# Moving the attention of two token chunks later, and the gate's quadratic into its accumulator banks, in a fused attention and two-layer FFN kernel

## The chip, the core and the metric

The kernel runs on one core of a Trainium2 chip. The metric is the device time of one execution in microseconds (us), the median of several runs. TensorE (PE) multiplies matrices and writes PSUM, which has eight banks of 128x512 f32; VectorE (DVE), ScalarE (ACT) and GpSimd (POOL) do the rest; SyncE (SP) issues the DMAs.

## The reference, cut to what matters

```python
def _attn_ref(q, k, v, f_logit):              # 4 x 8 x 768 x 48
    f = 1.0 / (1.0 + np.exp(-f_logit))
    for t in range(S):
        state = f[:, :, t, :, None] * state + np.einsum('bhd,bhe->bhde', k[:, :, t], v[:, :, t])
        y[:, :, t] = np.einsum('bhd,bhde->bhe', q[:, :, t], state)

def _moe_ref(x, w_in, w_out, a, b):           # 3072 x 384 -> 2048 -> 384
    h = x @ w_in
    P = a[0] + a[1] * h + a[2] * h2 + a[3] * h3       # h2 = h*h, h3 = h2*h
    Q = 1.0 + np.abs(b[0]) * np.abs(h) + np.abs(b[1]) * h2
    return (P / (Q + 1e-06)) @ w_out

def _moe2_ref(x, domain_probs, w1, w2):       # 4 experts, 384 -> 1024 -> 384
    p = domain_probs / (domain_probs.sum(-1, keepdims=True) + 1e-09)
    for e in range(E):
        h = np.maximum(x @ w1[e], 0.0)
        out += p[:, e:e + 1] * (h @ w2[e])
```

A linear attention with a decaying state feeds a first FFN, whose activation is the quotient P/Q (the "gate"). Its result feeds a second FFN with four experts.

## The kernel before, in words

The 3072 tokens are cut into six chunks of 512 (c = 0 to 5), each of four blocks of 128 tokens (b = 0 to 3, one per batch row). The program is one loop over steps v (from -25 to 192). Chunk c's second FFN fills the 32 steps 32c to 32c+31 (four experts of eight tiles). A step holds, in this order on PE: "in2" of tile v+1 (9 matmuls, line L863, into one of two banks hb), "out2" of tile v-1 (9 matmuls, L873, summed in three banks acc), and, where the tables say so, a tile of the next chunk's first FFN: "in1" (9 matmuls into bank 5, called h1) and, four times a chunk, "out1" (36 matmuls, L873, into the same banks acc). All matrices are split into a high and a low part, hence three products for each.

Around them: relu(v) makes the high part of a tile on ACT (L983) and the low part on DVE (L984). With two hb banks, in2(v+2) at the start of step v+1 has to wait for L984 of tile v. gate_in is on ACT: a copy of the bank (L929), its square q (L933), r (L934) and y (L935). gate_step is on DVE, for the tile before (L944, L946 or L953, L958, L975) and for the new one (L949, L968, L970), with a Ln and an Exp on ACT (L950, L951) and a cast on ACT (L960). At the end of an expert evac2 takes the three acc banks (L1018 on DVE, L1019 on POOL); out1 follows it in the same banks, and evac1 adds its result (L1036). In the first steps, until about step 33, ACT and POOL also split weights into high and low parts (L819, L820).

The attention of chunk c, block b runs in six stages, in the steps t0(c, b)+1 to t0(c, b)+6. First stage: a decay on DVE (w, L431, and four scans, L438). Second: its inverse on ACT (L446, L447), the scaled key on POOL (L452), and a Newton correction on DVE (L457, L458, L462). Third: the scaled query on POOL (L467). Fourth: the scores on PE (L471) and their mask on DVE (L482). Fifth: L487 and L495 on PE. Sixth: the state's update on PE (L538), and L552 and L564 on DVE. From chunk 1's tiles on, the attention uses banks 6 and 7. When a chunk is finished, write_out transposes four blocks on PE (L1043), copies each on ACT (L1050) into one of two buffers (os), and sends it out by a DMA (L1052).

Nothing is reordered by a scheduler: each engine executes its instructions in the order in which this loop writes them. What sets that order are the numbers in first_mix_steps and t0.

Of the kernel before, what the change touches and what calls it, by code (L numbers as in the profile page):

```python
# [8 lines left out]
F32 = mybir.dt.float32  # L9
# [8 lines left out]
NB, NH, S, D = 4, 8, 768, 48  # L18
DM = NH * D
C = 128  # L20
NCH = S // C
# [324 lines left out]
def first_mix_steps():  # L346


    when, groups = {}, {}
    for c in range(1, NCH):  # L350
        p = NE * NJ2 * (c - 1)
        if c == 1:
            at = [10, 11, 12, 13, 14, 15, 16, 17, 18, 19, 20, 21, 23, 24, 25, 26]
            ends = (16, 20, 24, 29)
        else:
            at = [2, 3, 4, 5] if c == 2 else [-1, 1, 3, 5]
            at += [7, 9, 11, 13, 15, 17, 19, 21, 23, 24, 25, 26]
            ends = (8, 16, 24, 29)
        for j, s in enumerate(at):
            when[p + s] = (c, j)  # L360
        for n, s in enumerate(ends):
            groups[p + s] = (c, n)
    return when, groups
# [204 lines left out]
class Att:  # L568
# [16 lines left out]
    @staticmethod  # L585
    def t0(c, b):
        if c == 1:
            return -6 + 3 * b
        if c == 2:
            return (8, 14, 20, 26)[b]  # L590
        return NE * NJ2 * (c - 1) - (30, 24, 17, 9)[b]

    def start(self, fetch):
# [103 lines left out]
    def begin(self, v):  # L697
        ops = tuple([] for _ in range(7))
        for c in range(1, NCH):
            for b in reversed(range(NB)):  # L700
                k = v - self.t0(c, b)
                if 1 <= k <= 6:
                    for at, fs in self.stage(self.blocks[c, b], k).items():
                        ops[at].extend(fs)
        return ops
# [3 lines left out]
def fused(ctx, tc, aps, consts, gm, big, dp, prep, flag_op):  # L709
# [8 lines left out]
    acc, hb, h1 = banks[0:3], banks[3:5], banks[5]  # L718
# [206 lines left out]
    def gate_in(u):  # L925
        h = u[2]
        if u[0]:
            h = gp.tile([128, 512], F32, tag="h", name="h")
            nc.scalar.copy(out=h, in_=u[2])  # L929
        q = gp.tile([128, 512], F32, tag="q", name="q", bufs=3) if u[0] else banks[5 + u[1] % 2]  # L930
        r = gp.tile([128, 512], F32, tag="r", name="r")
        y = gp.tile([128, 512], F32, tag="y", name="y")
        nc.scalar.activation(out=q, in_=h, func=AF.Square)  # L933
        nc.scalar.activation(out=r, in_=h, func=AF.Abs, scale=sc[:, 4:5])  # L934
        nc.scalar.activation(out=y, in_=h, func=AF.Identity, scale=sc[:, 0:1], bias=sc[:, 1:2])  # L935
        return q, r, y, h
# [104 lines left out]
    def write_out(c, b, bank):  # L1041
        for m in range(3):
            nc.tensor.transpose(bank[:, m * C:(m + 1) * C], o[c][:, m, b * C:(b + 1) * C], ident)  # L1043
        if c == NCH - 1:
            if not last:
                last.append(sp.tile([128, NB, DM], F32, tag="s1", name="os"))
            nc.scalar.copy(out=last[0][:, b], in_=bank[:, 0:DM])
            return
        t = osp.tile([128, DM], F32, tag="os", name="os")
        nc.scalar.copy(out=t, in_=bank[:, 0:DM])  # L1050
        r0 = b * S + c * C
        nc.sync.dma_start(out=out[r0:r0 + C, :], in_=t)  # L1052
# [12 lines left out]
    for v in range(-FILL - 6, LAST + 1):  # L1065
        tau = v + FILL
        ops = att.begin(v)
        if tau == -4:
            prep()
        if tau + 6 <= NB:  # L1070
            att.first(tau + 6, conv_ops(tau), fetch, partial(fill_in, 0, 0, NB - 1))
        run_late()
        store_all()
        items = steps.get(v, [])
        lead = 1 if items and items[0][0] == "in2" and items[0][1] == v + 1 else 0
        fill_run(ops[PA], 9 * lead)
        for item in items[:lead]:
            emit(item)
        if 0 <= v < LAST and v not in act2:
            relu(v)  # L1080
        for f in ops[ACT0]:
            f()
        for u in gate_queue:
            if u[0] and u[:2] not in gate:
                gate[u[:2]] = gate_in(u)
        if 0 <= tau + 1 < NJ1:
            fill_in(tau + 1, (NB - 1) * (tau < 0))
        ready = [u for u in gate_queue if u[:2] in gate]
        new = ready[0] if ready else None
        if new:  # L1090
            gate_queue.remove(new)
        old, pend_old = pend_old, new
        if new or old:
            gate_step(new, old, ops)
        else:
            for f in ops[DVE1] + ops[ACT1] + ops[POOL1]:
                f()
        c, k = v // (NE * NJ2) - 1, v % (NE * NJ2)
        if v in (LAST - 4, LAST - 3):
            for b in range(2):  # L1100
                write_out(NCH - 1, b + 2 * (v - LAST + 4), banks[6 + b])
        if 0 <= c < NCH - 1 and k == 2:
            for b in range(2):
                write_out(c, b + (2 if c else 0), banks[6 + b])
        fill_run(ops[PB], 9 * any(item[0] == "out2" for item in items), True)
        for item in items[lead:]:
            if item[0] == "out2":
                emit(item)
                if run_bounds(v - 1)[1]:
                    evac2(v - 1)  # L1110
        for item in items[lead:]:
            if item[0] == "in2":
                emit(item)
                if v + 1 < LAST:
                    relu(v + 1)
        if 0 <= c < NCH - 1 and k == (1 if c else 2):
            for b in range(2):
                write_out(c, b + (0 if c else 2), banks[6 + b])
        for item in items[lead:]:
            if item[0] == "out1":  # L1120
                emit(item)
        for item in items[lead:]:
            if item[0] == "in1":
                emit(item)
        for u in gate_queue:
            if not u[0] and u[:2] not in gate:
                gate[u[:2]] = gate_in(u)
        if tau == -1:
            spread_probs()
        if 0 <= tau - 2 < NJ1:  # L1130
            fill_out(tau - 2)
        for f in ops[REST]:
            f()
        if v in groups:
            evac1(*groups[v])
        if tau + 6 > NB:
            for f in sum(conv_ops(tau), []):
                f()
            run_late()
        if 10 <= tau and v < -1:  # L1140
            make_ready(min(R - 6, 2 * (tau - 9)))
            split_to(min(AHEAD, state["ready"] - 2))
        if tau == NJ1 + 1:
            for m in range(3):
                split_x2(0, m, acc[m], nc.vector)
            load_pb(0)
        if v >= -1:
            split_to(state["used"] + AHEAD)
        att.loads(v)
        if v == 170:  # L1150
            flag_op(banks[6], banks[7])
# [178 lines left out]
```

## Time and profile before

| | us |
|---|---|
| median of 3 runs | 1368.79 (1368.64 to 1369.47) |
| the profiled execution | 1367.35 |
| its span in the trace | 1365.5 |
| PE busy in the span | 1325.7 (97%) |
| DVE busy | 870.5 (64%) |
| ACT busy | 663.1 (49%) |
| POOL busy | 287.6 (21%) |

The profiled execution took 1.85 us around its span, and was 1.44 us under the median. A row of the trace's timeline gives the start, the duration, the engine, the line, what is written from what, the count, and in brackets how long the engine had been idle and what it waited for. Line numbers are those of the kernel before.

### The profile page before, as it was taken

The numbers are of one execution on the slowest core, as the hardware profiler recorded it, in microseconds if no ns is written. First come the engines' busy times: TensorE is split into PE (matmuls) and PEld (weight loads), VectorE is DVE, ScalarE is ACT, GpSimd is POOL, SyncE is SP. The second block draws the span as 40 slices with busy tenths as digits, with TensorE's granted clock in tenths as the row PEclk, the third lists the DMA queues.
The fourth block names the chain that finished last, engine by engine and source line by source line (L and its number), as shares of the span: only waits on it lengthen the run. The fifth ranks groups of instructions, "written<-read, shape, count | busy, mean of one in ns | idle before, by whom it ended". The sixth has DMA issues, their size and how long they took to land.

```text
span 1365.5 us, 19581 instructions
## 1 busy us (share of the span) xinstructions
PE 1325.7 (97%) x7152; PEld 1060.7 (78%) x7152; DVE 870.5 (64%) x1367; ACT 663.1 (49%) x1152; POOL 287.6 (21%) x257
## 2 busy tenths in 40 slices
PE   7899999898899999999999999999999999999998
PEld 6444788777788888888888888888888888888887
DVE  7999659677748576757666757576575465552221
ACT  3897448666536545525545535553445453431111
POOL 0133555566420020120110111001111000111010
PEclk9999999999999999999999999999999999999999
DMA  8547877667875666667656758665657676667660
GB/s 298 199 174 260 284 259 263 223 242 254 301 255 176 207 219 189 188 207 228 221 166 204 227 166 267 198 208 186 216 176 243 191 196 195 192 192 239 195 195 28
DMA packets 115706, 291.03 MB, mean 213 GB/s; under 512 B 13105, under 2 KB 28817, under 8 KB 114833
## 3 DMA queue, kind: packets, MB, share of 16 engines
q1 hardware_dynamic: 115024, 289.51, 65.9%
q8 instruction: 59, 0.97, 0.3%
q14 instruction: 47, 0.38, 0.1%
q10 hardware_dynamic: 576, 0.18, 0.1%
HBM read 240.83 MB, written 48.81 MB: 212 GB/s over the span
## 4 chain that ended last, share of the span: by engine, by line


## 5 line engine op out<-in xcount | busy, mean ns | idle before, releaser
L863 PE MATMUL bank<-x,w 128*128 128x512 f32 x2448 | 595.1, 391 | 6.7 <-DVE gl L984 6.7
L863 PEld LDWEIGHTS bank<-x,w 128*128 128x128 f32 x2448 | 457.2, 188 | 103.9 <-DVE gl L984 8.8
L873 PE MATMUL bank<-gh,w 128*128 128x512 f32 x1584 | 495.0, 394 | 6.6 <-DVE t L1018 6.6
L873 PEld LDWEIGHTS bank<-gh,w 128*128 128x128 f32 x1584 | 295.5, 189 | 73.2 <-DVE t L1018 7.9
L873 PE MATMUL bank<-gl,w 128*128 128x512 f32 x792 | 309.8, 391 | 0.0
L984 DVE SCALAR_TENSOR_TENSOR gl<-bank,gh 128x512 fp32r<-128x512 f32 x192 | 131.4, 685 | 154.5 <-ACT gh L983 154.2
L1019 POOL TENSOR_TENSOR o<-o,t 128x512 f32<-128x512 f32 x69 | 88.9, 1317 | 529.1 <-DVE t L1018 529.1
L873 PEld LDWEIGHTS bank<-gl,w 128*128 128x128 f32 x792 | 149.3, 189 | 31.3
L983 ACT ACTIVATE gh<-bank 128x512 fp32r<-128x512 f32 x192 | 113.7, 593 | 122.6 <-PE bank L863 122.6
L949 DVE SCALAR_TENSOR_TENSOR q<-q,sc,r 128x512 f32<-128x512 f32 x80 | 61.6, 770 | 141.8 <-ACT r L934 141.8
L960 ACT CAST gh<-q 128x512 fp32r<-128x512 f32 x80 | 49.2, 615 | 186.7 <-DVE q L958 186.6
L820 POOL TENSOR_TENSOR w<-rawbuf,w 128x384 fp32r<-128x384 f32 x96 | 104.5, 1113 | 88.6 <-ACT w L819 74.2
L929 ACT COPY h<-bank 128x512 f32<-128x512 f32 x80 | 46.8, 585 | 114.6 <-PE bank L863 113.9
L1036 DVE TENSOR_TENSOR s<-s,bank 128x512 f32<-128x512 f32 x45 | 31.0, 688 | 84.5 <-PE bank L873 84.4
L975 DVE TENSOR_TENSOR gl<-q,gh 128x512 fp32r<-128x512 f32 x80 | 55.9, 699 | 33.8 <-ACT gh L960 33.6
L950 ACT ACTIVATE r<-q,sc 128x512 f32<-128x512 f32 x80 | 58.0, 725 | 25.1 <-DVE q L949 18.4
L944 DVE SCALAR_TENSOR_TENSOR q<-q,r 128x512 f32<-128x512 f32 x80 | 69.5, 868 | 0.1
L935 ACT ACTIVATE y<-h,sc 128x512 f32<-128x512 f32 x80 | 64.2, 803 | 0.0
L958 DVE SCALAR_TENSOR_TENSOR q<-y,sc,q 128x512 f32<-128x512 f32 x80 | 62.2, 778 | 1.8
L970 DVE SCALAR_TENSOR_TENSOR y<-y,sc,h 128x512 f32<-128x512 f32 x80 | 61.1, 764 | 2.8
L951 ACT ACTIVATE r<-r 128x512 f32<-128x512 f32 x96 | 60.7, 633 | 3.0
L968 DVE TENSOR_TENSOR y<-y,h 128x512 f32<-128x512 f32 x80 | 57.2, 716 | 0.0
(113 smaller groups left out, 1220.5 us busy)
## 6 DMA issues: line engine op xcount, KB each, us to landing
w<-ws SPq DMA_DIRECT2D x448, 384.0 KB, 3.6
ws<-w SPq DMA_DIRECT2D x96, 384.0 KB, 4.1
raw<-in_w_dram SPq DMA_DIRECT2D x16, 768.0 KB, 6.3
rawbuf<-in_w_dram SPq DMA_DIRECT2D x64, 192.0 KB, 3.9
v<-in_v_dram SPq DMA_DIRECT2D x24, 320.0 KB, 4.8
f<-in_qkf_dram SPq DMA_DIRECT2D x24, 256.0 KB, 4.0
k<-in_qkf_dram SPq DMA_DIRECT2D x24, 256.0 KB, 4.3
q<-in_qkf_dram SPq DMA_DIRECT2D x24, 256.0 KB, 4.6
```

The lines of the kernel that those rows point to most:

```text
L820: nc.gpsimd.tensor_tensor(out=t[:, 1], in0=r, in1=t[:, 0].bitcast(F32), op=ALU.subtract)
L863: nc.tensor.matmul(ps, a[:, o], b[:, kk, :], start=(n == 0), stop=(n == 8))
L873: nc.tensor.matmul(acc[m], a[:, o], b, start=(start and n == 0), stop=(stop and n == last))
L935: nc.scalar.activation(out=y, in_=h, func=AF.Identity, scale=sc[:, 0:1], bias=sc[:, 1:2])
L944: vec.scalar_tensor_tensor(out=q0, in0=q0, scalar=QC, in1=r0, op0=ALU.add, op1=ALU.mult)
L949: vec.scalar_tensor_tensor(out=q, in0=q, scalar=sc[:, 5:6], in1=r, op0=ALU.mult, op1=ALU.add)
L951: nc.scalar.activation(out=r, in_=r, func=AF.Exp, scale=-1.0)
L958: vec.scalar_tensor_tensor(out=q0, in0=y0, scalar=sc[:, 3:4], in1=q0, op0=ALU.subtract, op1=ALU.mult)
L970: vec.scalar_tensor_tensor(out=y, in0=y, scalar=sc[:, 2:3], in1=h, op0=ALU.subtract, op1=ALU.mult)
L983: nc.scalar.activation(out=gh, in_=h, func=AF.Relu)
L984: nc.vector.scalar_tensor_tensor(out=gl, in0=h, scalar=0.0, in1=gh.bitcast(F32), op0=ALU.max, op1=ALU.subtract)
L1019: nc.gpsimd.tensor_tensor(out=o[c][:, m], in0=o[c][:, m], in1=t, op=ALU.add)
```

## The change

The tables of numbers change in three places. (1) Chunk 2's sixteen in1 tiles stand in steps 42 to 53 and 55 to 58, one in each, instead of every second step from 34 on, with out1 in steps 48, 52, 56 and 61 instead of 40, 48, 56 and 61. Chunk 3's first four stand in 65, 66, 67 and 69 instead of 63, 65, 67 and 69. (2) The attention of chunk 2 starts at 20, 25, 30 and 35 instead of 8, 14, 20 and 26, and that of chunk 3 at 42, 47, 52 and 57 instead of 34, 40, 47 and 55. (3) The gate's q of chunk 1's tiles 0 to 8 (steps 10 to 19) lies in bank 6 or 7, by turns, instead of in SBUF. The four transposes of chunks 1 to 4 all stand in one step (the third of the next chunk), where two stood in the step before; those of chunk 0 use bank 5 and are spread over two steps.

```diff
-        if c == 1:
+        if c < 3:
             at = [10, 11, 12, 13, 14, 15, 16, 17, 18, 19, 20, 21, 23, 24, 25, 26]
             ends = (16, 20, 24, 29)
         else:
-            at = [2, 3, 4, 5] if c == 2 else [-1, 1, 3, 5]
+            at = [1, 2, 3, 5] if c == 3 else [-1, 1, 3, 5]
...
         if c == 2:
-            return (8, 14, 20, 26)[b]
+            return 20 + 5 * b
+        if c == 3:
+            return 42 + 5 * b
...
-            for b in reversed(range(NB)):
+            for b in reversed(range(NB)) if c == 1 else range(NB):
...
-        q = gp.tile([128, 512], F32, tag="q", name="q", bufs=3) if u[0] else banks[5 + u[1] % 2]
+        q = gp.tile([128, 512], F32, tag="q", name="q", bufs=3) if u[0] > 1 or u[0] and u[1] > 8 else banks[5 + u[0] + u[1] % 2]
...
-        if 0 <= c < NCH - 1 and k == 2:
+        if c == 0 and k in (2, 3):
+            write_out(c, 2 * k - 4, h1)
+        if 0 < c < NCH - 1 and k == 2:
             for b in range(2):
-                write_out(c, b + (2 if c else 0), banks[6 + b])
+                write_out(c, b, banks[6 + b])
...
-        if 0 <= c < NCH - 1 and k == (1 if c else 2):
+        if c == 0 and k in (2, 3):
+            write_out(c, 2 * k - 3, h1)
+        if 0 < c < NCH - 1 and k == 2:
             for b in range(2):
-                write_out(c, b + (0 if c else 2), banks[6 + b])
+                write_out(c, b + 2, banks[6 + b])
```

Where the instructions stand, first on DVE in step 16, from relu's L984 (L986 after; the lines behind the change count two more) to the evacuation ahead of the first out1. Before:

```order
L984 SCALAR_TENSOR_TENSOR gl<-bank_95,gh 128x512
L944 SCALAR_TENSOR_TENSOR q<-q,r 128x512
L946 SCALAR_TENSOR_TENSOR q<-q,r 128x512
L949 SCALAR_TENSOR_TENSOR q<-q,sc,r 128x512
L958 SCALAR_TENSOR_TENSOR q<-y,sc,q 128x512
L968 TENSOR_TENSOR y<-y,h 128x512
L970 SCALAR_TENSOR_TENSOR y<-y,sc,h 128x512
L457 SCALAR_TENSOR_TENSOR i<-g,bank_98 112x512
L458 TENSOR_TENSOR gm<-gm,g 112x4
L975 TENSOR_TENSOR gl<-q,gh 128x512
L1018 TENSOR_TENSOR t<-bank_92,pb 128x512
```

The same place after the change:

```order
L986 SCALAR_TENSOR_TENSOR gl<-bank_95,gh 128x512
L946 SCALAR_TENSOR_TENSOR bank_98<-bank_98,r 128x512
L948 SCALAR_TENSOR_TENSOR bank_98<-bank_98,r 128x512
L951 SCALAR_TENSOR_TENSOR bank_99<-bank_99,sc,r 128x512
L960 SCALAR_TENSOR_TENSOR bank_98<-y,sc,bank_98 128x512
L970 TENSOR_TENSOR y<-y,h 128x512
L972 SCALAR_TENSOR_TENSOR y<-y,sc,h 128x512
L977 TENSOR_TENSOR gl<-bank_98,gh 128x512
L1020 TENSOR_TENSOR t<-bank_92,pb 128x512
```

The Newton correction (L457, L458) is gone from ahead of the evacuation, and q is a bank.

Second, DVE in steps 53 and 54 (the third chunk's tiles, and the fourth chunk's attention). Before, step 53 from its L984 to that of step 54:

```order
L984 SCALAR_TENSOR_TENSOR gl<-bank_96,gh 128x512
L944 SCALAR_TENSOR_TENSOR q<-q,r 128x512
L953 SCALAR_TENSOR_TENSOR q<-q,r 128x512
L958 SCALAR_TENSOR_TENSOR q<-y,sc,q 128x512
L552 TENSOR_TENSOR x<-bank_99,x 128x3x128
L975 TENSOR_TENSOR gl<-q,gh 128x512
L564 TENSOR_TENSOR am_4756<-bank_98,s_2_141 48x192 x2
L984 SCALAR_TENSOR_TENSOR gl<-bank_95,gh 128x512
```

After, from the gate's L951 of step 53 to the first gate instruction of step 54:

```order
L951 SCALAR_TENSOR_TENSOR q<-q,sc,r 128x512
L960 SCALAR_TENSOR_TENSOR q<-y,sc,q 128x512
L970 TENSOR_TENSOR y<-y,h 128x512
L972 SCALAR_TENSOR_TENSOR y<-y,sc,h 128x512
L552 TENSOR_TENSOR x<-bank_99,x 128x3x128
L431 TENSOR_SCALAR bank_99<-f 112x512
L977 TENSOR_TENSOR gl<-q,gh 128x512
L559 TENSOR_TENSOR am_4583<-bank_98,s_1_140 48x192 x2
L438 SCALAR_TENSOR_TENSOR g<-bank_99,sc 112x128 x4
L986 SCALAR_TENSOR_TENSOR gl<-bank_95,gh 128x512
L946 SCALAR_TENSOR_TENSOR q<-q,r 128x512
```

Step 53 gained a whole new tile's part of the gate and the first stage of another block.

Third, ACT around the transposes of chunk 1 (L1050 copies a transposed block, L1052 after). Before, steps 65 and 66:

```order
L960 CAST gh<-q 128x512
L1050 COPY os<-bank_98 128x384
L1050 COPY os<-bank_99 128x384
L983 ACTIVATE gh<-bank_95 128x512
L929 COPY h<-bank_97 128x512
L933 ACTIVATE q<-h 128x512
L934 ACTIVATE r<-h,sc 128x512
L935 ACTIVATE y<-h,sc 128x512
L950 ACTIVATE r<-q,sc 128x512
L951 ACTIVATE r<-r 128x512
L1050 COPY os<-bank_98 128x384
L1050 COPY os<-bank_99 128x384
```

After, step 66 and the start of 67:

```order
L952 ACTIVATE r<-q,sc 128x512
L953 ACTIVATE r<-r 128x512
L1052 COPY os<-bank_98 128x384
L1052 COPY os<-bank_99 128x384
L1052 COPY os<-bank_98 128x384
L1052 COPY os<-bank_99 128x384
L985 ACTIVATE gh<-bank_96 128x512
L425 ACTIVATE f<-f 112x512
L931 COPY h<-bank_97 128x512
```

The four copies follow one another, with no gate's or relu's work between the pairs.

## Rows read from the trace of the kernel before

**Rows 1.** The head of the page: the span.

```profile
span 1365.5 us, 19581 instructions
```

**Rows 2.** Windows of 40 us: busy us (x count) of each engine, PE's clock.

```profile
280.00:320.00 40.00, 35.98 (x166) 28.26 (x165) 30.46 (x46) 23.67 (x45) 24.48 (x22) 1.00 0.70 244
320.00:360.00 40.00, 36.05 (x212) 29.27 (x211) 33.22 (x48) 25.74 (x48) 23.50 (x21) 1.00 0.83 293
360.00:400.00 40.00, 38.88 (x242) 31.80 (x241) 15.90 (x27) 9.49 (x19) 14.36 (x13) 1.00 0.75 255
400.00:440.00 40.00, 39.49 (x238) 32.13 (x237) 33.87 (x54) 27.84 (x48) 2.67 (x3) 1.00 0.66 206
```

**Rows 3.** Waits of PE: us, times, longest.

```profile
PE bank L863 <- DVE gl L984: 6.7, 5, 2.5
PE bank L873 <- DVE t L1018: 6.6, 3, 4.2
...
PE bank L1043 <- POOL o L1019: 2.2, 3, 0.8
...
PE bank L487 <- DVE am L482: 0.5, 1, 0.5
```

**Rows 4.** PE's timeline, around steps 27 to 28.

```profile
344.38 4.24 PE L863 MATMUL bank<-x,w 128*128 128x512 f32 x18
348.46 0.61 PE L873 MATMUL bank<-gh,w 128*128 128x512 f32 x2
...
357.21 2.37 PE L863 MATMUL bank<-x,w 128*128 128x512 f32 x9 [2.47 <-DVE gl L984]
```

**Rows 5.** PE's timeline, first matmuls of out1 in step 16.

```profile
244.21 1.22 PE L873 MATMUL bank<-gh,w 128*128 128x512 f32 x2 [4.24 <-DVE t L1018]
```

**Rows 6.** A window of 6.8 us behind it, columns as in group 2.

```profile
242.80:249.60 6.80, 5.39 (x13) 4.29 (x14) 6.15 (x10) 2.31 (x6) 5.37 (x4) 0.50 0.00 1
```

**Rows 7.** DVE's timeline, steps 15 and 16.

```profile
233.63 0.69 DVE L431 TENSOR_SCALAR bank<-f 112x512 f32<-112x512 f32 x1
...
235.06 1.35 DVE L438 TENSOR_TENSOR_SCAN g<-bank,sc 112x128 f32<-112x128 f32 x4
...
237.63 1.67 DVE L946 SCALAR_TENSOR_TENSOR q<-q,r 128x512 f32<-128x512 f32 x1
...
242.19 0.68 DVE L457 SCALAR_TENSOR_TENSOR i<-g,bank 112x512 f32<-112x512 f32 x1
...
243.47 1.88 DVE L1018 TENSOR_TENSOR t<-bank,pb 128x512 f32<-128x512 f32 x3
```

**Rows 8.** Groups by line and form: count, busy us, mean ns.

```profile
L944 DVE SCALAR_TENSOR_TENSOR q<-q,r 128x512 f32<-128x512 f32 x80 | 69.5, 868 | 0.1
...
L944 DVE SCALAR_TENSOR_TENSOR bank<-bank,r 128x512 f32<-128x512 f32 x16 | 11.1, 692 | 0.1
```

**Rows 9.** DVE's timeline, starts of the gate in steps 57 to 59.

```profile
555.10 0.69 DVE L944 SCALAR_TENSOR_TENSOR q<-q,r 128x512 f32<-128x512 f32 x1
...
563.63 1.40 DVE L944 SCALAR_TENSOR_TENSOR q<-q,r 128x512 f32<-128x512 f32 x1
...
569.61 0.68 DVE L944 SCALAR_TENSOR_TENSOR q<-q,r 128x512 f32<-128x512 f32 x1
```

**Rows 10.** ACT's timeline, chunk 0's third and fourth copy.

```profile
399.69 0.95 ACT L1050 COPY os<-bank 128x384 f32<-128x384 f32 x2 [4.45 <-DMA out_dram<-os]
```

**Rows 11.** The line L1052: its DMAs from issue to landing.

```profile
DMA to landing us min/median/max: 1.9/3.7/5.9
```

**Rows 12.** DVE's timeline, relu of tile 37.

```profile
415.30 0.68 DVE L984 SCALAR_TENSOR_TENSOR gl<-bank,gh 128x512 fp32r<-128x512 f32 x1
```

**Rows 13.** PE's timeline, in1 of step 37 and in2 of step 38.

```profile
415.74 4.24 PE L863 MATMUL bank<-x,w 128*128 128x512 f32 x18
```

**Rows 14.** ACT's timeline, chunk 2's second pair of copies, in step 98.

```profile
834.05 0.84 ACT L1050 COPY os<-bank 128x384 f32<-128x384 f32 x2
```

**Rows 15.** PE's timeline, behind out2 of the same step.

```profile
834.34 2.21 PE L863 MATMUL bank<-x,w 128*128 128x512 f32 x9
```

## The prediction

> **What bounds the kernel now.** I read the windows of 40 us first. From 400 us on PE is at work nearly all the time (39.49 of 40), at full clock; between 280 and 400 us it stands still for 4.02, 3.95 and 1.12 us a window [rows 2]. So the end is set by PE, which has a fixed number of matmuls to do, and only what makes PE wait or lowers its clock can be gained or lost. The list of PE's waits says what these are [rows 3]: L863 for the low part of the relu (L984), five times; L873 for the evacuation (L1018), three times, one of 4.2 us; L1043 (transposes) for POOL's sum, 2.2 us in three; and L487 once, 0.5 us. A run of 18 matmuls starts at 344.38 and what follows it at 348.46 [rows 4], so a matmul is 0.227 us, nine are 2.04, a step with in2, out2 and in1 is 6.12, one without in1 4.08, and an out1 8.17.
>
> All sums are made against the profiled execution, 1367.35 us (the span of 1365.5 [rows 1] and 1.85 around it). The median shown is 1.44 above it, and I add that at the end.
>
> **Step 16.** [...] On DVE stand ahead of L1018, with no idle time among them, the first stage of the attention (L431 from 233.63, 0.6; the scans from 235.06, 1.28), and the Newton correction (0.68 with what follows it); L946 takes 1.67 [rows 7]. The change takes the first two away from here, 2.56 us, and puts q into a bank. L944 costs 868 ns on average with q in SBUF and 692 with q in a bank (chunk 0's tiles) [rows 8]; the undisturbed one in SBUF is 0.69 too [rows 9], so what the bank saves is not the instruction's own time but the stretch that it is held up. For L946 I take 1.0 (1.67 against 0.69; bounds 0 and 1.0). Together 3.5 of the 4.24; I leave 0.8 of the wait, since ACT has the gate and the weights' casts to do in the same steps and is then last, and no low clock behind it: -3.4 - 2.6 = **-6.0** (bounds -6.8, the whole, and -3, if ACT holds it and the clock falls all the same).
>
> [...]
>
> **Steps 20 to 24.** Here are 4.02 us of idle time in the window 280 to 320, and 1.48 behind it (3.95 less 2.47) [rows 2, 4]. The attention is in the same stages in steps 21 to 24 as before, only that it is block 0 and not block 2, and from tile 9 on q is in SBUF as before. What is gone is the last stage of another block in step 20. I take **-1.1** (bounds -3.5 and +0.5).
>
> **Steps 26 to 29.** The second block starts at 25 where the fourth started at 26, so its first stage (1.87 us of DVE by [rows 7]) stands in step 26, a full step with a block's last stage in it, and its second stage in step 27. What a second stage costs DVE is read where no weights are split any more: step 57 goes from 555.10 to 563.63, 8.53 us, the next, with a third stage, takes 5.98 [rows 9]. Before, the wait at the start of the step behind it is 2.47 us, for L984 [rows 4], and one of 1.1 follows (the idle time of 360 to 400 [rows 2]). Now L984 comes later by 1.87 to 2.55 (8.53 less 5.98), less what DVE recovers while it waits for ACT's gate; I take 1.8 more: one wait of 4.3 instead of 2.47 and 1.1, +0.7. The clock stayed at 1.00 over the 2.47 [rows 2] and fell behind the 4.24 [rows 6]; at 4.3 I count three quarters of the 2.56, +1.9. Sum **+2.6** (bounds -1.5 and +5).
>
> **Steps 42 to 61.** Here the third chunk's tiles, one in each step, meet the fourth chunk's attention, where before they had two steps each and PE had no idle time in the windows. I follow DVE from the start of step 53 (0). Its gate begins at about 2.1, behind three or four instructions of ACT (an estimate). The step has the first stage: 5.98 - 0.70 (the hold-up of L944, 1.40 against 0.69 [rows 9]) + 1.87 = 7.15, so L984 of tile 54 is done at 9.2; PE wants it at 9.1 (4.08, since a tile of in2 came early in step 52, 0.9 for the state's update, 4.08 for step 54 which has no in1): 0.1. Step 54 with the second stage adds 7.9 to 8.53: 17.1 against 9.2 + 6.12 = 15.3: 1.8. In step 56 the evacuation is reached after 6.0 for the third stage and 2.6 for four instructions, 25.7; PE gets there at 17.1 + 1.2 (scores) + 3 x 2.04 = 24.5: 1.2. Steps 58 to 61 repeat the arrangement that gave 2.47 and 1.1 in steps 27 to 29, without splits: 2.0. Sum **+5.1** (bounds +1 and +9: nothing but the last, or 8.53 for every second stage and the groups at 48 and 52 too).
>
> **Transposes.** The three waits for POOL's sum (2.2 us [rows 3]) are gone, as the sums are long done a step later. But the second pair now follows the first by one out2 and needs the same banks: in step 98 ACT copies at 834.05 for 0.84 [rows 14], and PE is through with out2 at 834.34 [rows 15], so a wait of some 0.4, three times, +1.2. And the third copy needs an output buffer whose DMA has not landed (3.7 us, up to 5.9 [rows 11]): chunk 0 had this arrangement already, and ACT waited 4.45 us [rows 10]. Behind it stand the next relu and gate. There the relu of tile 37 was done at 415.98, and PE wanted it at 417.78 [rows 12, 13]: 1.8 to spare. In step 70 the spare is less by 2.04 (step 68 has no in1) and by 1.3 (two DVE instructions of the gate of tile 65): 1.5 of wait. Steps 98 to 102 have the same with one tile less, 1.2; step 130 has no attention behind it, 0.2; step 162 no gate. Sum -2.2 + 1.2 + 1.5 + 1.2 + 0.2 = **+1.9** (bounds -2.2 and +6).
>
> **The rest.** The 0.5 us of L487 in step 39 [rows 3] has no counterpart, **-0.5**. One more evacuation in step 52 (three instructions of DVE and POOL) lies beside the matmuls of out2 and in2.
>
> Sum: -6.0 - 1.1 + 2.6 + 5.1 + 1.9 - 0.5 = +2.0: 1369.35 for an execution like the profiled one, 1370.8 as a median. Less than 0.2% (2.7 us) can hardly be told from no change.
>
> **The rivals.** *Less held up, faster.* If q in a bank keeps DVE and POOL from holding each other up in steps 10 to 20, POOL's splits also run earlier, and steps 21 to 28 find DVE quieter: the long instructions there (as the 1.67) become short ones. Then steps 20 to 24 give -3.5 and 26 to 29 -1.5, and with half of the third chunk's waits (+2.5, DVE's spare time between the groups suffices) the sum is -7.1: 1361.7. For it: L944's two means. Against: tiles 9 to 15 keep q in SBUF. It decides if DVE's step 27 takes under 7 us. *Low clock in the third chunk, slower.* If the 1.8 of step 54 and 1.2 of step 56 become waits longer than the 2.47 over which the clock held, PE falls to its lower level twice, 2 x 2.6 more: 1376.0. For it: the same stages in steps 22 to 24 already gave a largest wait of about 2 us. Against: no splits here. [...]
>
> **How the numbers follow.** The likeliest case, the sum above, has 0.50, with its own range 1366.5 to 1375; of it about 0.01 is faster by over 0.2%, 0.31 within, 0.18 slower, as 1371.5 is close to its middle. Less held up: 0.24. Low clock in the third chunk: 0.18. The bank gives nothing: 0.08, 0.01 of it within. So faster 0.25, within 0.2% 0.32, slower 0.43. The range reaches to the middle of the outer two, 1362 to 1377, which leaves out 0.12 of the first and under 0.08 of the others.
>
> **What would show it.** In the profile after: no wait at the first out1 of step 16 over 1 us, and clock 1.00 behind it; L944 and L946 with a bank at about 0.69; a wait for L984 of about 4 us at the start of step 29, with a clock under 1 behind it; idle time of PE of 4 to 6 us in steps 53 to 61 (some 500 to 590 us), for L984 and L1018; no wait of L1043 for POOL, but short ones for ACT, and ACT waiting four to five us for output DMAs in four steps, with a PE wait of 1 to 2 us two steps behind two of them. The prediction is wrong if steps 53 to 61 have no idle time (then it is faster by 3 us), or if the low clock appears where I counted none.

## The result, and the profile after

The changed kernel takes 1375.73 us (median of 6 runs, 1374.5 to 1375.88) against 1368.72 of the kernel before (6 runs on the same chip): a ratio of 1.0053, with a 95% interval of 1.0042 to 1.0064. It is slower by half a per cent, 7 us. The prediction had 1370.8, with 1362 to 1377 as its range and 0.43 for slower. The profiled execution took 1375.88 us, with a span of 1374.1; that is 8.5 us over the profiled execution of the kernel before, so the pair of traces differs by 1.5 us more than the medians do.

The list of PE's waits (microseconds, times, the longest), of the changed kernel, in which line numbers are two higher:

```profile
PE bank L865 <- DVE gl L986: 11.8, 7, 4.7
...
PE bank L875 <- DVE t L1020: 4.3, 5, 2.1
...
PE bank L1045 <- ACT os L1052: 1.9, 2, 1.0
```

Beside [rows 3]: the wait for the evacuation lost its big piece (6.6 to 4.3, the longest 4.2 to 2.1), the waits for POOL's sum and for L487 are gone, and the waits for the relu's low part went from 6.7 to 11.8 us, with a longest of 4.7. PE's timeline of the changed kernel shows where they are; in brackets the idle time and what ended it:

```profile
237.25 0.73 PE L875 MATMUL bank<-gh,w 128*128 128x512 f32 x2 [0.66 <-DVE t L1020]
...
272.28 0.73 PE L875 MATMUL bank<-gh,w 128*128 128x512 f32 x2 [2.09 <-DVE t L1020]
...
300.75 1.50 PE L865 MATMUL bank<-x,w 128*128 128x512 f32 x3 [2.04 <-DVE gl L986]
...
347.30 1.22 PE L865 MATMUL bank<-x,w 128*128 128x512 f32 x2 [4.66 <-DVE gl L986]
...
537.08 1.20 PE L865 MATMUL bank<-x,w 128*128 128x512 f32 x4 [1.40 <-DVE gl L986]
...
545.62 0.72 PE L875 MATMUL bank<-gh,w 128*128 128x512 f32 x2 [0.79 <-DVE t L1020]
...
579.47 0.73 PE L865 MATMUL bank<-x,w 128*128 128x512 f32 x2 [1.86 <-DVE gl L986]
...
642.22 0.96 PE L865 MATMUL bank<-x,w 128*128 128x512 f32 x3 [1.30 <-DVE gl L986]
```

The first row is out1 of step 16: 0.66 us where 4.24 stood [rows 5]. Then come step 20's out1, the starts of steps 24 and 29, the start of step 55, out1 of step 56, the start of step 61, and step 70. How the clock went is read from windows of 10 us over the same places (the third number from the end is PE's granted clock):

```profile
270.00:280.00 10.00, 7.91 (x28) 6.19 (x28) 5.00 (x9) 5.20 (x12) 7.69 (x8) 0.83 0.41 140
300.00:310.00 10.00, 9.25 (x43) 6.93 (x43) 7.11 (x11) 6.15 (x12) 4.64 (x5) 0.83 0.62 217
340.00:350.00 10.00, 5.34 (x18) 4.02 (x17) 9.89 (x13) 3.81 (x7) 5.17 (x4) 0.77 0.75 250
350.00:360.00 10.00, 10.00 (x51) 7.88 (x50) 5.45 (x10) 2.42 (x5) 5.84 (x5) 0.89 0.80 275
580.00:590.00 10.00, 10.00 (x49) 7.89 (x48) 7.31 (x11) 1.60 (x3) 3.94 (x4) 0.83 0.30 97
```

In the kernel before, the clock was lower in one place between step 10 and the last few microseconds, that of [rows 6]; now it is in four, each behind a wait of 1.86 us or more. A window of 10 us at 0.83 has lost 1.7 us of full clock, and the five together have 8.5. Not all of that is taken from matmuls. Ahead of step 29 the clock is down while PE still waits:

```profile
346.00:347.00 1.00, 0.00 (x0) 0.00 (x0) 1.00 (x3) 0.00 (x0) 1.00 (x2) 0.50 0.72 286
```

About 1.0 of the 3.4 us at this place lie ahead of the first matmul at 347.30, so the matmuls lost 2.4.

Term by term, from the two traces (the waits, and the clock that the matmuls lost, in both kernels without the part that lies within a wait):

| place | forecast | waits | clock | measured |
|---|---|---|---|---|
| step 16 | -6.0 | 4.24 to 0.66 | -2.6 | -6.2 |
| steps 20 to 24 | -1.1 | 5.5 to 4.7 | +3.4 | +2.6 |
| steps 26 to 29 | +2.6 | 3.6 to 4.7 | +2.4 | +3.5 |
| steps 42 to 61 | +5.1 | 0 to 4.05 | +1.7 | +5.8 |
| transposes | +1.9 | 2.2 to 3.6 | 0 | +1.4 |
| step 39 | -0.5 | 0.5 to 0 | 0 | -0.5 |
| before step 0 | 0 | | | +1.1 |
| sum | +2.0 | | | +7.7 |

The sum is 0.8 short of the 8.5 us of the two profiled executions; where the 0.8 lie is not shown. The 1.1 us ahead of step 0 (the first relu on DVE starts at 140.35 before and 141.41 after) is no effect of the change: in the twelve kernels below, which all have the same beginning, it starts between 139.91 and 141.97.

### The profile page after: what moved, and what is told of

It is laid out like the page before. It is cut to its first block, busy times and chain, and to the rows that moved or that the text cites. A ratio compares the mean times of both kernels' runs of the same rounds, so it can differ in the third digit from the quotient of the medians.

```text
span 1374.1 us, 19595 instructions
## 1 busy us (share of the span) xinstructions
PE 1330.0 (97%) x7152; PEld 1061.9 (77%) x7152; DVE 860.1 (63%) x1370; ACT 661.5 (48%) x1152; POOL 283.7 (21%) x260
## 4 chain that ended last, share of the span: by engine, by line
## 5 line engine op out<-in xcount | busy, mean ns | idle before, releaser
L865 PE MATMUL bank<-x,w 128*128 128x512 f32 x2448 | 600.5, 393 | 12.1 <-DVE gl L986 11.8
L986 DVE SCALAR_TENSOR_TENSOR gl<-bank,gh 128x512 fp32r<-128x512 f32 x192 | 131.4, 685 | 171.5 <-ACT gh L985 171.4
L1021 POOL TENSOR_TENSOR o<-o,t 128x512 f32<-128x512 f32 x72 | 91.9, 1305 | 517.3 <-DVE t L1020 517.3
L951 DVE SCALAR_TENSOR_TENSOR q<-q,sc,r 128x512 f32<-128x512 f32 x71 | 55.1, 776 | 117.6 <-ACT r L936 117.6
L822 POOL TENSOR_TENSOR w<-rawbuf,w 128x384 fp32r<-128x384 f32 x96 | 98.9, 1060 | 96.3 <-ACT w L821 89.6
L962 ACT CAST gh<-q 128x512 fp32r<-128x512 f32 x71 | 43.6, 614 | 154.9 <-DVE q L960 154.9
L977 DVE TENSOR_TENSOR gl<-q,gh 128x512 fp32r<-128x512 f32 x71 | 49.0, 690 | 30.1 <-ACT gh L962 29.9
L946 DVE SCALAR_TENSOR_TENSOR q<-q,r 128x512 f32<-128x512 f32 x71 | 64.4, 907 | 0.0
L952 ACT ACTIVATE r<-q,sc 128x512 f32<-128x512 f32 x71 | 51.5, 725 | 22.8 <-DVE q L951 16.7
L1020 DVE TENSOR_TENSOR t<-bank,pb 128x512 f32<-128x512 f32 x72 | 46.8, 685 | 19.5 <-PE bank L875 19.1
L936 ACT ACTIVATE r<-h,sc 128x512 f32<-128x512 f32 x80 | 56.6, 708 | 0.0
```

What stands on the lines that cost most here:

```text
L822: nc.gpsimd.tensor_tensor(out=t[:, 1], in0=r, in1=t[:, 0].bitcast(F32), op=ALU.subtract)
L865: nc.tensor.matmul(ps, a[:, o], b[:, kk, :], start=(n == 0), stop=(n == 8))
L946: vec.scalar_tensor_tensor(out=q0, in0=q0, scalar=QC, in1=r0, op0=ALU.add, op1=ALU.mult)
L951: vec.scalar_tensor_tensor(out=q, in0=q, scalar=sc[:, 5:6], in1=r, op0=ALU.mult, op1=ALU.add)
L986: nc.vector.scalar_tensor_tensor(out=gl, in0=h, scalar=0.0, in1=gh.bitcast(F32), op0=ALU.max, op1=ALU.subtract)
L1021: nc.gpsimd.tensor_tensor(out=o[c][:, m], in0=o[c][:, m], in1=t, op=ALU.add)
```

## The experiments

My theory before them: the sum is right about the waits, and its error is the lower clock, which now also stands behind waits of about 2 us, and step 20. All were timed in turns with the kernel before, whose median was 1368.0 to 1368.5 in these series. Differences below are against the changed kernel's 1375.73; it was timed only in its own series, where the kernel before had 1368.72, so up to 0.7 us of a difference can be the series'.

**The banks taken back (x_qsbuf).** Only q's place is undone:

```diff
-        q = gp.tile([128, 512], F32, tag="q", name="q", bufs=3) if u[0] > 1 or u[0] and u[1] > 8 else banks[5 + u[0] + u[1] % 2]
+        q = gp.tile([128, 512], F32, tag="q", name="q", bufs=3) if u[0] else banks[5 + u[1] % 2]
```

> The changed kernel with the gate's q of the second chunk's tiles in SBUF again, as before; all else as changed. Theory: what frees step 16 is that no attention stands there any more; the bank saves about 1 us a step only, and in steps 17 to 20 ACT sets the pace. So the wait of out1 in step 16 grows from 0.66 to about 1.7 us at most, that of step 20 stays near 2, and the time is that of the changed kernel within 2 us (1375 to 1378). Rival (the banks do the work): the wait in step 16 comes back with 3 us or more and the lower clock behind it, 1380 or more. [...]

Measured: 1382.31 us (ratio to before 1.0107, 1.0094 to 1.0121), 6.6 us more than the changed kernel. My expectation was wrong; the rival that the banks do the work holds. PE's timeline at the first out1 and at that of step 20:

```profile
240.40 1.22 PE L875 MATMUL bank<-gh,w 128*128 128x512 f32 x2 [3.65 <-DVE t L1020]
...
280.03 1.22 PE L875 MATMUL bank<-gh,w 128*128 128x512 f32 x2 [3.67 <-DVE t L1020]
```

Though no attention stands in steps 10 to 20, the wait in step 16 is 3.65 us, and a smaller one of 0.46 stands ahead of it: together 4.1, nearly the 4.24 of the kernel before. The clock falls behind it, as the rival had it: a window of 10 us has 0.72. Why is read from the groups of DVE's instructions in steps 10 to 16 (count, busy us, mean ns). Of this kernel:

```profile
L948 DVE SCALAR_TENSOR_TENSOR q<-q,r 128x512 f32<-128x512 f32 x5 | 7.0, 1393 | 0.2
```

Of the changed kernel:

```profile
L948 DVE SCALAR_TENSOR_TENSOR bank<-bank,r 128x512 f32<-128x512 f32 x5 | 3.5, 700 | 0.2
```

One instruction of the gate takes twice as long with q in SBUF, in every step. It runs in part beside POOL's split of weights (in step 15 from 227.90, POOL's from 225.24 to 228.75), whose instructions are longer too (1191 ns on average against 1018); in the changed kernel it does so as well (from 226.29, POOL's to 226.64) and takes 0.70 us. Why it is this one, and not L946 ahead of it (0.75 us, all of it beside the split), is not shown. DVE's L951, queued behind it, comes late, and ACT's Ln waits for that, and behind the Ln stand ACT's casts and the next relu. So the 0.7 us go round a ring of three engines. Its period is read from one relu to the next on DVE's timeline. Here:

```profile
226.51 0.69 DVE L986 SCALAR_TENSOR_TENSOR gl<-bank,gh 128x512 fp32r<-128x512 f32 x1 [1.04 <-ACT gh L985]
...
233.66 0.69 DVE L986 SCALAR_TENSOR_TENSOR gl<-bank,gh 128x512 fp32r<-128x512 f32 x1 [1.04 <-ACT gh L985]
```

and in the changed kernel, steps 19 and 20 (the same 6.32 us stand between the relus of steps 13 to 16):

```profile
259.98 0.69 DVE L986 SCALAR_TENSOR_TENSOR gl<-bank,gh 128x512 fp32r<-128x512 f32 x1 [1.00 <-ACT gh L985]
...
266.30 0.69 DVE L986 SCALAR_TENSOR_TENSOR gl<-bank,gh 128x512 fp32r<-128x512 f32 x1 [0.99 <-ACT gh L985]
```

A step lasts 7.15 us with q in SBUF and 6.32 with q in a bank; PE's part is 6.12. The lag of 1.03 a step collects over four steps and falls due at the out1 behind them: 4.1. It is nearly the wait of the kernel before, whose steps held the stages of the attention besides. The gate's other instructions on DVE differ little between the two places: L951 has 753 ns with banks and 742 without, L946 690 and 733.

**The transposes taken back (x_trback).** Chunks 1 to 4 as before:

```diff
         if 0 < c < NCH - 1 and k == 2:
             for b in range(2):
-                write_out(c, b, banks[6 + b])
+                write_out(c, b + 2, banks[6 + b])
...
-        if 0 < c < NCH - 1 and k == 2:
+        if 0 < c < NCH - 1 and k == 1:
             for b in range(2):
-                write_out(c, b + 2, banks[6 + b])
+                write_out(c, b, banks[6 + b])
```

> The changed kernel with the transposes of chunks 1 to 4 where they stood before (a pair in the second step, a pair in the third). Theory: the two PE waits for ACT's copies (1.9 us) and the 1.6 us of waits in steps 69 and 70 go, the three waits for POOL's sum (2.2 us) come back: 1.4 us less, about 1374.4. Rival (the waits in steps 69 and 70 come from the tiles in steps 65 to 67, not from the copies held up by the output DMA): these 1.6 us stay, and the time does not fall (1375.7 to 1376.2).

Measured: 1371.89 us (1.0029, 1.0018 to 1.0041), 3.8 less. In the trace the waits in steps 69 and 70 are gone, as the theory had it, and the waits of steps 65 to 130 are 1.45 us where they were 3.58: 2.1 less, since only two of the three waits for POOL came back. The rest is at other places, where the clock stays up: behind step 24 (1.00 from 300 to 310 us, where the changed kernel has 0.83), in part behind step 29 (0.83 and 1.00 from 340 to 360 us, there 0.77 and 0.89), and in step 20. PE's timeline in step 20, and the window behind it:

```profile
272.53 0.73 PE L875 MATMUL bank<-gh,w 128*128 128x512 f32 x2 [2.10 <-DVE t L1020]
```

```profile
270.00:280.00 10.00, 7.89 (x35) 6.20 (x34) 5.61 (x9) 5.53 (x12) 7.45 (x7) 1.00 0.41 143
```

The code there is the same and so is the wait, 2.10 us, but the clock stays at 1.00 (35 matmuls in the window against 28). So the lower clock behind a wait of this length is not given by the wait alone, and a kernel's time carries it as a gain or a loss of some 2 us that its edit has nothing to do with. It differs between executions of one kernel, too: of this kernel's seven, three took 1370.3 to 1370.7 us with a mean clock of 0.992 or 0.993, and four 1371.9 to 1373.1 with 0.989 to 0.991. The trace is of one of the three. So how much of the 3.8 us belongs to the edit is not shown beyond the 2.1 of the waits.

**Idle time filled (x_warm).** Matmuls whose result nobody reads go ahead of the waits, into a bank that is free:

```diff
+    def keep_busy(v, bank, at):
+        for _ in range(at.get(v, 0)):
+            x = x2[v // (NE * NJ2)]
+            nc.tensor.matmul(bank, x[:, 0, 0, 0:C], x[:, 0, 0, :], start=True, stop=True)
...
+        keep_busy(v, banks[7], {24: 8, 29: 18, 61: 7})
         fill_run(ops[PA], 9 * lead)
...
+        keep_busy(v, h1, {20: 8})
         for item in items[lead:]:
             if item[0] == "out1":
```

> The changed kernel with matmuls whose result nobody reads put ahead of the four waits behind which the clock was lower: 8 ahead of out1 in step 20, and 8, 18 and 7 ahead of in2 at the start of steps 24, 29 and 61, each about as long as the wait. Theory: the waits are idle time of PE that brings the lower clock, and with work in them the granted clock stays at 1.00; the lower clock cost 1.7, 1.7, 3.4 and 1.7 us by the windows, so the time falls by about 8, to 1367 to 1369. Rival (the clock falls for another reason, or the extra matmuls end later than what they wait for): the windows behind them still show 0.6 to 0.85, and the time is 1375 to 1379.

Measured: 1371.00 us (1.0021, 1.0012 to 1.0030), 4.7 less. Two windows behind the longest wait, whose counterparts in the changed kernel had 0.77 and 0.89:

```profile
340.00:350.00 10.00, 9.40 (x52) 7.29 (x51) 9.21 (x13) 4.50 (x9) 3.95 (x4) 1.00 0.74 258
350.00:360.00 10.00, 10.00 (x45) 7.96 (x44) 5.69 (x10) 1.80 (x5) 5.67 (x5) 1.00 0.77 274
```

The clock is at 1.00 in every window of 10 us from step 0 to 700 us, so idle time is what lowers it at these four places, and the rival falls. But 4.7 is not 8. Laid beside the changed kernel, PE is ahead by 1.63 us at step 24's out1, still by 1.56 at step 29, by 3.45 at step 56. The slower matmuls behind step 24 cost nothing, as PE would only have waited longer for DVE in the same steps (0.34 and 1.51 here, 0.56 there), and those behind step 29 cost 1.9 of the 2.4 that the matmuls lost there. So the loss of clock in a stretch where another engine is late is a bound, not a price.

**Six casts earlier (x_act).** In step 16 ACT splits ahead as far as the ring of weights allows:

```diff
-            split_to(state["used"] + AHEAD)
+            split_to(state["used"] + (R if v == 16 else AHEAD))
```

> The changed kernel with six of ACT's weight casts of steps 17 and 18 (and POOL's part of them) made in step 16, where ACT has spare time beside out1. Theory: in steps 17 to 20 ACT is the engine that is last (about 6.3 us a step against PE's 6.12), so that out1 in step 20 waits for it through the gate; with 6 x 0.43 us less ACT work there the wait of 2.09 us shrinks below 0.5 and the lower clock behind it goes: 3 to 4 us less, 1372 to 1373. Rival (DVE's own queue ahead of the evacuation is what is late): the wait stays near 2 us and the time at 1375.7.

Measured: 1373.82 us (1.0052, 1.0038 to 1.0066), 1.9 less, which is not clear of the changed kernel's interval; the wait of step 20 is 1.88 against 2.09, and a new one of 1.24 stands in step 17. Neither theory had that. The relus of steps 18 and 19 on DVE:

```profile
255.66 0.68 DVE L986 SCALAR_TENSOR_TENSOR gl<-bank,gh 128x512 fp32r<-128x512 f32 x1
...
260.89 0.68 DVE L986 SCALAR_TENSOR_TENSOR gl<-bank,gh 128x512 fp32r<-128x512 f32 x1
```

Without casts the period is 5.23 us and DVE has no idle time: so ACT did set the 6.32, as I had said. But the casts in a row held the gate of step 17 up (the last waited 0.76 us for its data), and DVE had to make that good until step 20. For the question of step 20 it is inconclusive.

**Three casts earlier (x_act2).**

```diff
-            split_to(state["used"] + AHEAD)
+            split_to(state["used"] + AHEAD + 3 * (v in (16, 17, 18, 20, 21, 22, 24, 25, 26)))
```

> The changed kernel with three of ACT's weight casts of step 19 (and POOL's part of them) made in step 16 beside out1, three of step 23 made in step 20, and three of steps 27 and 28 made in step 24. Six at once, tried before, held the gate of step 17 up, since their data was not there yet; three are made without such a wait if the theory holds. Theory: in steps 17 to 19 a step lasts 6.32 us on ACT (from one relu to the next) where the run with six casts less had 5.23, so without casts in step 19 out1 of step 20 waits 0.9 instead of 2.09, and the wait of 2.04 before step 24 and of 4.66 before step 29 shrink by up to 1 us each: 2 to 4 us less with what the clock gives back, 1372 to 1373.5. Rival (DVE's queue is what is late): the waits stay as they are within 0.3 us and the time stays at 1375.7, or falls to 1372 with the clock alone, at unchanged waits.

Measured: 1378.33 us (1.0076, 1.0062 to 1.0089), 2.6 more. ACT's timeline in step 18:

```profile
258.60 0.52 ACT L821 CAST w<-rawbuf 128x384 fp32r<-128x384 f32 x1
261.89 1.00 ACT L821 CAST w<-rawbuf 128x384 fp32r<-128x384 f32 x2 [2.78 <-DMA rawbuf<-w1s]
```

A cast three ahead of its turn waits 2.78 us for the DMA of its weights, and the relu queued behind it with it. So ACT's casts in these steps can't be moved that way, and how much step 20's wait is worth without them stays open.

**The third chunk's attention one step later (x_t28).**

```diff
-            return 20 + 5 * b
+            return (20, 26, 31, 36)[b]
...
+            if c == 2:
+                at = [11, 12, 13, 14, 15, 16, 17, 18, 19, 20, 21, 22, 24, 25, 26, 27]
```

> The changed kernel with the third chunk's attention blocks 1, 2 and 3 one step later (starting at 26, 31 and 36) and, since its tiles need them, the third chunk's tiles one step later too (43 to 54, 56 to 59). Theory: the wait of 4.66 us before step 29 is there because a block's first stage stands in step 26 beside a full tile and the last stage of another, and its second in step 27 beside the gate of the last tile; a step later, DVE has 2 us less ahead of it, the wait is about 2.5 (as before the change, with one of 1.1 behind it) and the clock falls less: 3 us less at this place, 1372 to 1373.5 if the third chunk's waits stay. Rival (the wait is set by how many stages stand in steps 26 to 29 together, in whatever order): 1375.7 and a wait of over 4 us, perhaps one step later.

Measured: 1373.37 us (1.0033, 1.0021 to 1.0045), 2.4 less. PE's timeline around steps 29 and 30:

```profile
342.70 2.35 PE L867 MATMUL bank<-x,w 128*128 128x512 f32 x9 [2.46 <-DVE gl L988]
...
348.23 2.11 PE L867 MATMUL bank<-x,w 128*128 128x512 f32 x8 [1.14 <-DVE gl L988]
```

These are the waits of the kernel before to 0.04 us (2.47 [rows 4] and 1.1), and as there the clock stays at 1.00. So the place of the second block's first two stages, in steps 26 and 27, was the cause of the 4.66. The third chunk's waits, now 5.5 us instead of 4.05, took part of it back.

**The fourth chunk's attention one step earlier (x_c3m1), and its last block one step later (x_c3b58).**

```diff
-            return 42 + 5 * b
+            return 41 + 5 * b
```

> The changed kernel with all four attention blocks of the fourth chunk one step earlier (41, 46, 51, 56). Theory: the waits in steps 55, 56 and 60 (1.4, 0.8 and 1.9 us, and the lower clock behind the last, 1.7) come from the second stage standing in a step without a tile, where PE has only 4.08 us of work; a step earlier, the third block's first stage lies beside out1 of step 52 and its second in a full step, and the fourth block's second in step 58, a full one: 3 to 5 us less, 1371 to 1373. Rival (DVE has too much to do over these steps, wherever the stages stand): the same sum of waits at other steps, 1375 to 1377.

Measured: 1375.51 us (1.0050, 1.0037 to 1.0063). No gain: the rival holds. The list of PE's waits:

```profile
PE bank L875 <- DVE t L1020: 7.8, 5, 3.3
```

The waits in steps 55, 56 and 61 became one of 3.3 us in step 48, ahead of the first out1 of this chunk, one of 1.45 and one of 0.4: 5.15 in all, where 4.05 stood. The clock is at 1.00 in the windows of 10 us over all three. PE's timeline at the longest, and the window of 10 us around it:

```profile
474.98 0.73 PE L875 MATMUL bank<-gh,w 128*128 128x512 f32 x2 [3.30 <-DVE t L1020]
```

```profile
470.00:480.00 10.00, 6.70 (x30) 5.25 (x29) 9.49 (x14) 3.87 (x7) 4.99 (x4) 1.00 0.25 83
```

The other shift,

```diff
-            return 42 + 5 * b
+            return (42, 47, 52, 58)[b]
```

> The changed kernel with the last attention block of the fourth chunk one step later (58 instead of 57). Theory: DVE's backlog before step 61 comes from the block's first two stages in steps 58 and 59, which both have a tile's gate; in 59 and 60 the second has none, some 1.4 us less on DVE: the wait of 1.86 us goes below 0.6 and with it the lower clock behind it, 1.4 to 3 us less, 1372.7 to 1374.3. Rival (as with all four blocks earlier: the waits only move): a wait of 1.5 us or more in steps 59 to 63, and 1375 to 1376.5.

gave 1371.94 us (1.0032, 1.0019 to 1.0044), 3.8 less, more than was expected, though the wait only went to 1.08. PE's timeline at step 62:

```profile
581.60 1.67 PE L865 MATMUL bank<-x,w 128*128 128x512 f32 x6 [1.08 <-DVE gl L986]
```

The clock is at 1.00 behind it. 0.8 of wait and 1.7 of clock explain 2.5 of the 3.8; in the profiled execution the difference is 3.5, 1.5 of it ahead of step 0.

**Four output buffers (x_os4).**

```diff
-        t = osp.tile([128, DM], F32, tag="os", name="os")
+        if b < 2:
+            t = osp.tile([128, DM], F32, tag="os", name="os")
+        else:
+            t = tp.tile([128, 512], F32, tag="t", name="t")[:, 0:DM]
```

> The changed kernel with four output buffers instead of two (the second pair of blocks is copied into two of the evacuation's buffers, free at that time). Theory: ACT's third copy waits 4 to 5 us for an output DMA, and the relu and gate behind it are what PE waits for in steps 69 and 70 (1.6 us): ACT's waits for output DMAs are gone and so are these, 1.5 us less, about 1374. PE's two waits of 1 us for ACT's copies in steps 98 and 130 stay. Rival (the extra tile in step 66 and the attention in step 67 alone make them): PE's waits there stay, no change (1375.2 to 1376).

Measured: 1372.52 us (1.0028, 1.0019 to 1.0037), 3.2 less. In the changed kernel ACT's list of waits has

```profile
ACT os L1052 <- DMA out_dram<-os: 9.0, 4, 3.8
```

and here it has no wait for an output DMA (one of 3.8 us for a DMA stands at a copy, put down to the weights' w<-ws). The waits in steps 69 and 70 are gone with it, those for ACT's copies in steps 98 and 130 (1.9 us) stay: the theory holds at this place (1.6 us). In the profiled execution the clock is up besides (1.00 in the windows from 270 to 310 us, where the changed kernel has 0.83 twice) behind about the same waits, 2.09 and 2.02 us in steps 20 and 24. That the other 1.6 us of the median come from there is likely and not shown: the executions of this kernel lie between 1370.7 and 1374.5.

**Both together, and what came of it (x_trwarm, x_best, x_final).** The transposes as before and the idle time filled, in one kernel (the edits above):

> The changed kernel with the transposes of chunks 1 to 4 where they stood before, and the matmuls nobody reads ahead of the waits in steps 20, 24, 29 and 61. Each alone gave 3.8 and 4.7 us less than the changed kernel. Theory: they act on different waits, but both of them also took away lower clock behind a wait, so less than the sum: the waits of steps 66 to 130 are 2.1 us less by the trace, and the clock at 1.00 gives 4.7: 1368.5 to 1370, that is, the kernel before within its uncertainty. Rival (nothing in common): 8.5 less, 1367.

Measured: 1366.85 us, a ratio to the kernel before of 0.9988 (0.9980 to 0.9997): faster by 0.12%, less than the 0.2% that I had set as what can be told. The two edits add up fully, as the rival had it: 8.9 us less, against 3.8 and 4.7. Its list of PE's waits:

```profile
PE bank L875 <- DVE t L1020: 3.5, 5, 1.5
PE bank L865 <- DVE gl L986: 3.0, 6, 1.4
PE bank L1045 <- POOL o L1021: 1.4, 2, 0.7
```

The waits are short because matmuls stand in them: DVE is no quicker from one relu to the next (6.07 us behind the wait of step 24, 6.05 in the changed kernel). Adding the casts of x_act2, the last block at 58 and fewer filling matmuls:

> The kernel with transposes where they stood before and idle time filled (1366.85, the fastest so far), with the casts three steps ahead and the last block at 58, and fewer filling matmuls to fit (3, 6 and 14). If these two shorten the waits as expected (1 us in step 20, up to 1 in 24 and 29, 1.4 in 61): 1362 to 1365, clear of the kernel before. If the casts and the block change nothing: 1366 to 1369.

Measured: 1371.35 us (1.0028, 1.0018 to 1.0037); the casts' wait for DMA is in it, as in x_act2. With 6 matmuls ahead of step 24 instead of 8, a wait of 2.94 us was left there, and the clock fell behind it:

```profile
290.00:300.00 10.00, 7.06 (x27) 5.44 (x26) 9.50 (x14) 6.23 (x12) 5.41 (x5) 0.88 1.03 398
```

Without the casts, and with 8 and 18 filling matmuls again and 4 in step 62:

> The kernel with the transposes where they stood before and the idle time filled, with the fourth chunk's last block at 58 and the casts where the change has them (8 filling matmuls in step 20, 8, 18 and 4 at the start of steps 24, 29 and 62). Theory: the block alone took the wait of 1.86 us to 1.08 and the lower clock away; the clock is held up by the filling anyway, so only the 0.8 us are left to gain on 1366.85: 1365.5 to 1366.5, 0.15% under the kernel before. Rival (the two add up): 1363.

Measured: 1368.35 us, a ratio of 1.0000 (0.9990 to 1.0009). The block at 58 gains nothing more once the clock is held, and neither theory's number came; the time is 1.5 us over that of x_trwarm, and why is not shown.

## Why the prediction was right, and where it was wrong

**The way and the range** were right, the point was 4.9 us short. The likeliest case had its own range up to 1375, and the result lies 0.7 above it. It lies next to the rival with low clock in the third chunk (1376.0) by luck: that rival wanted waits over 2.47 us in steps 54 and 56, and the waits at the starts of 55 and in 56 stayed at 1.40 and 0.79 with the clock at 1.00 behind them. The lower clock came in steps 20, 24 and 61, for which no rival stood, and by the sign that the prediction set itself (a lower clock where none was counted) it was wrong there. That 1362 to 1377 still held the result is owed to the width of the range and not to the account of the clock.

**Less held up, the rival with 0.24**, fell. It wanted DVE's step 27 under 7 us; from relu to relu DVE takes 8.87 and 9.76 us in the steps ahead of the wait at step 29, and 9.60 stood there before.

**Step 16** was right in its size (-6.0 forecast, -6.2 in the trace) and wrong in its reason. I gave 2.56 of it to the stages of the attention that leave and 1.0 to the bank (and read DVE as never idle there; one gap of 0.18 us stands at 239.48). With the stages gone and q in SBUF the wait is 3.65 and 0.46, hardly less than before: with the stages gone, the bank makes the whole of the gain. What it would do beside them was not run. The 2.6 of clock in this term, and the 2.56 of which the term of steps 26 to 29 takes three quarters, are the loss behind the wait of [rows 5]: 12 matmuls took 5.28 us there, at 0.50 [rows 6], where 12 of 0.227 take 2.72. It is gone, with 1.00 from 238 to 246 us. I had read the right row, L946 at 1.67 us [rows 7], but priced it once, in step 16, where it comes in every step and runs round through ACT (7.15 us a step against 6.32).

**Steps 20 to 24** were the step that failed: I took -1.1, and it is +2.6. The waits did fall, by 0.8, though within them step 20's rose from 0.9 to 2.09; why it rose stays open (x_act and x_act2). What I put at nothing is the clock, which can fall behind waits of this size: 3.4 us by the windows, of which the filled kernel shows some 1.6 on the path. The inference "held over 2.47, fell behind 4.24" took one row each for a limit. In the changed kernel it fell behind 2.09, 2.04 and 1.86.

**Steps 26 to 29**: the mechanism was right, and x_t28 shows it. The forecast was one wait of 4.3 with 1.9 of clock; it is 4.66 with 2.4 lost by the matmuls, 1.9 of it on the path. The term was undersized by 0.4 of wait and 0.5 of clock. A reading under it was wrong: the 8.53 us of step 57 [rows 9], taken for what a second stage costs DVE, hold 1.92 us in which DVE stood idle for ACT. In the kernel before:

```profile
558.43 0.75 DVE L949 SCALAR_TENSOR_TENSOR q<-q,sc,r 128x512 f32<-128x512 f32 x1 [1.92 <-ACT r L934]
```

I took 1.8 for the delay of L984, under the 2.55 that this row had given, so that 4.3 came near is in part luck.

**Steps 42 to 61**: the waits forecast at steps 55, 56 and 61 were 1.8, 1.2 and 2.0; they are 1.40, 0.79 and 1.86, all at the steps named, the first with the same 8.53 in its working. The 0.1 ahead of them did not come. Clock of 1.7 behind the last makes the term 5.8 instead of 5.1.

**Transposes**: waits of 1.2 for the banks were forecast, 1.9 came, two and not three. The wait behind ACT's copies was forecast as 1.5 in step 70 and came as 1.6 in steps 69 and 70; x_os4 shows the output DMA as its cause. ACT's waits for these DMAs were forecast at four to five us in four steps; they are four of 9.0 us together, the longest 3.8. The same in steps 98 to 102 (1.2 forecast) did not come: 0.

**The bank gives nothing, the rival with 0.08**: it fell. By the groups of rows in steps 10 to 16 none of the gate's five instructions with q in a bank is dearer by more than 11 ns (L951, 753 against 742), L948 is cheaper by 693, and without the bank the kernel takes 6.6 us more.

## What to carry to other kernels

An instruction that is held up in every step of a loop through three engines is priced by what it adds to the loop's period, times the steps until the next point where PE must wait; not by its own length at that point: here 0.7 us more in L948 made the step 0.83 longer (7.15 against 6.32), 1.03 over PE's part, and 4.1 of wait after four steps. Ask for each long row whether it repeats.

When work is moved out of one crowded stretch into another, the waits that it makes there can be forecast by following the late engine's queue from the rows, here to within 0.4 us in four places; look for idle time inside the rows that are taken as an engine's cost. What is added on top is the clock: here it fell behind some waits of 1.86 us and held over one of 3.30, so count a possible loss as a range and not as a rule from one row, and only where PE, not another engine, is the last in the stretch that follows: in x_warm the clock held up behind step 24 saved nothing, that behind step 29 1.9 of the 2.4 us lost there.

An edit's measured gain may hold a change of the clock at a place that it doesn't touch. Compare the windows of the whole trace, and the clocks of the other executions, before a gain is put down to the edit.

## What the runs showed of the hardware that I had not expected

Behind the same wait in step 20, of the same code, the granted clock of the window was 0.83 in the changed kernel, in x_c3m1 and in x_c3b58 (waits of 2.09 us in all three), and 1.00 in x_trback, x_t28 and x_os4 (2.10, 2.11 and 2.09). It fell behind the 1.86 us of step 61 in all six kernels that have this wait, and held over 2.46 and 2.47 and over the 3.30 of x_c3m1. Behind 4.63 us and more, ahead of step 29, it fell in every kernel that did not fill the wait (the lower of the two windows of 10 us from 340 to 360 has 0.68 to 0.83). What decides it for the shorter ones is not settled by these runs. In x_warm and x_trwarm, where matmuls fill most of the idle time, the clock is at 1.00 in every window of 10 us from 140 to 700 us, and in x_final at 1.00 behind step 62 (580 to 590 us); in x_best, which left 2.94 us of one wait open, it fell to 0.88.

GpSimd's split of weights took 1191 ns on average in steps 10 to 16 with q in SBUF (x_qsbuf), against 1018 with q in a bank (the changed kernel).
